# Fused attention and feed-forward on one core: one load per twin of values, all second-product tiles in pairs, halved first loads and weights, and another order

## The chip, the core and the metric

The kernel runs on one NeuronCore of a Trainium2 chip. Its engines work side by side, each through its own list of instructions in order: TensorE (PE, with its weight loads as PEld), VectorE (DVE), ScalarE (ACT), GpSimd (POOL) and SyncE (SP, which here only issues DMA transfers). They wait for each other by semaphores. The metric is the device time of one execution in microseconds (us); the median of several runs counts. Less is better.

## The reference

Cosine attention over 8 batches, 12 heads, 448 positions of 64 numbers, whose output is the input of a feed-forward layer (3584 tokens of 768 numbers, 2048 inner ones) with a hard-swish between two matrix products:

```python
q_n = q / (np.linalg.norm(q, axis=-1, keepdims=True) + 1e-06)
k_n = k / (np.linalg.norm(k, axis=-1, keepdims=True) + 1e-06)
scores = np.matmul(q_n, k_n.transpose(0, 1, 3, 2)) / tau
attn = np.exp(scores - np.max(scores, axis=-1, keepdims=True))
attn = attn / (np.sum(attn, axis=-1, keepdims=True) + 1e-09)
x = np.matmul(attn, v)            # then heads side by side: 3584 x 768
h = x @ w_in
g = h * np.clip(h + 3.0, 0.0, 6.0) / 6.0
out = g @ w_out
```

## The kernel before

**Items and twins.** An item is a pair of heads (0 to 47, six to a batch); a twin is two items. `LQ.j` loads 448 KB of q or k for a twin into the big buffer; `SQ` squares it, `RE` sums the squares, `NO` makes the inverse norms of a twin on ACT (four short instructions), `NM` normalises into bf16, `TR` transposes on PE (the first 14 loads) or `XD` by DMA (later ones). `CQ`, `CK`, `CS` copy the transposed q and k to their places. `SC.i.g` makes the scores of group g of item i (three groups of two heads, and one, M, of the 64 left-over keys of both), `EX` takes the exponential on ACT, `VA` multiplies with the values, and `FI` divides by the sum, which comes from a column of ones beside the values. `BK`, `CX` (early) or `XB`, `XP` (by DMA) bring the result transposed into xT, the input of the first product. In the first six items the scores go through two buffers of their own (SC), later through a ring of six banks of PSUM (M, Y, Z) that the products use too.

**Values.** `LV.d` (load_v) brings the values of a twin: two groups of heads and two halves of the partitions, so four transfers of 64 partitions and 128 KB each, issued one after another by SP. Chunk 3 of the keys lies half in one place and half in another, and so both halves of the partitions are loaded four chunks wide, with one chunk in both. `VC.i` (vcast) turns an item's values into bf16 with one instruction of 128 partitions and 512 elements on POOL (L355), ACT (L355) or DVE (L353).

**First product.** `F.b.f` is one of 16 units per batch: six matmuls of 448 columns (L657); `FA` and `FV` apply the hard-swish on ACT and DVE (L666, L672) into gT. The last two batches' first product is done at the end in quarters with seven products for eight (`QA` to `QV`, L1039).

**Second product.** 28 tiles of 128 tokens. Tiles (0,0) and (0,1) are done alone by four units `T` (mm2_unit, L708), each 16 matmuls of 384 columns and a move `TE`. The other 26 are taken in 13 pairs with seven products of 8 matmuls each (product_unit, L850) for the eight that two tiles would take: `G` makes sums of activations (L825), `P` multiplies, `PE` moves a product out (tokens `PE` in the plan are moves; PE in the text is TensorE), `BO` (L881, L882) and `RS` (L885) add on POOL. `WS` makes the sums of the weights once. An "a" at the end of a token `P` gives the product a bank of its own; its parts are then added by `PL`.

**Weights.** `W.n` issues a transfer on POOL's queue: w_in in four pieces (two halves of the columns, two halves of the partitions), w_out in four.

**Order.** All of it stands in one table, PLAN: a list of tokens that is run through from the start and that gives each engine its order. `DP.n` in it are n dummy matmuls of zeros (busy_pv, L1157) that keep PE at work where it has nothing else. The number at the end of a token is a part of the work, and v, p, a name the engine. Before the plan, DVE and POOL set buffers: zeros beside the values, 12 small instructions for the columns of ones (L1203 to L1205), and zeros for the dummies.

Of the kernel before, what the change touches and what calls it, by code (L numbers as in the profile page):

```python
# [120 lines left out]
def kernel(  # L121
# [62 lines left out]
    def item(n):  # L184
        return big[:, n * RAW : (n + 1) * RAW].rearrange("p (g c d) -> p g c d", g=2, c=7)

    vr = [
        big[:, c : c + VAL].rearrange("p (i c d) -> p i c d", i=4, c=5)
        for c in range((NR + 2) * RAW, (NR + 2) * RAW + NV * VAL, VAL)
    ]  # L190
    NVX = 4
    vx = [const.tile([128, 8, D + 1], BF16, name=f"vx{i}", tag=f"vx{i}") for i in range(NVX)]
    raws = [item((i + 2) % NR) for i in range(NR)]
# [441 lines left out]
    def complete(b, t):  # L635
        assert t < 3 or b - 1 in left_done

    left_done = set()
    t_read = set()

    def g_left(b, e="v"):

# [610 lines left out]
```

## Time and profile before

| | |
|---|---|
| three runs | 400.4, 402.48, 401.76 us; median 401.76 |
| the profiled execution | 399.05 us, of which span 397.3 us from the first instruction to the last |
| granted TensorE clock | 0.999 |
| matmuls | 3796 |
| HBM read, written | 47.19 MB, 11.01 MB |
| q and k, one transfer | 448 KB, median 4.5 (q) and 5.2 us (k) to land |
| values, one of four | 128 KB, median 3.6 us to land |
| w_in, one of four | 768 KB, median 13.8 us to land |

How to read the lines of the profile that follow: the page gives each engine's busy time in us, its share of the span and its count of instructions. A line of the timeline gives start, length, engine, line of the kernel, operation, target and source, a count, and in brackets the idle time before it and what ended that. The chain of waits gives the pieces of the work that ended last, in order of time. Matmuls are pipelined and their ends modelled, so "busy" on PE is not peak work.

### The profile page before, as it was taken

To read this page: it belongs to the slowest core of one execution; us is meant where nothing else is said; L and a number is where in the kernel's file an instruction comes from. 1 tells how busy PE (TensorE), PEld (TensorE's weight loads), DVE (VectorE), ACT (ScalarE), POOL (GpSimd) and SP (SyncE) were. 2 spreads that over 40 slices of the span, in tenths; PEclk is the share of its full clock that TensorE was granted. 3 is DMA by queue.
4 is the path that set the end of the run, shared out by engine and by line. 5 is a ranking of instruction groups with operands and counts; after the bars stand their busy time and mean duration, and the time that the engine had idled before them with its cause. 6 is when DMAs were issued, how large, how long until landed. Compare 5 with 4: busy or idle time off the path is not lost.

```text
span 397.3 us, 10054 instructions
## 1 busy us (share of the span) xinstructions
PE 384.8 (97%) x3796; PEld 243.4 (61%) x3796; DVE 319.0 (80%) x565; ACT 282.8 (71%) x646; POOL 289.5 (73%) x257
## 2 busy tenths in 40 slices
PE   7789999999999999999999999999999999999995
PEld 6556565555655555655655655555556579977663
DVE  6969789898897779689879468867996798988773
ACT  5898998868777777886777766786875667744310
POOL 5879865394476988588369983879764898789492
PEclk9999999999999999999999999999999999999999
DMA  8998999998989798967975697775764750011224
GB/s 286 256 269 202 236 197 299 185 152 186 228 179 244 199 235 182 233 127 187 232 177 130 173 240 195 148 173 143 124 94 123 115 91 15 2 40 41 65 63 114
DMA packets 91569, 65.35 MB, mean 164 GB/s; under 512 B 56064, under 2 KB 89984, under 8 KB 91520
## 3 DMA queue, kind: packets, MB, share of 16 engines
q1 hardware_dynamic: 87408, 58.02, 63.8%
q0 software_dynamic: 3712, 6.29, 9.0%
q8 instruction: 29, 0.48, 0.5%
q10 hardware_dynamic: 400, 0.39, 0.3%
q14 instruction: 20, 0.16, 0.1%
HBM read 47.19 MB, written 11.01 MB: 146 GB/s over the span
## 4 chain that ended last, share of the span: by engine, by line
PE 86%; DVE 5%; ACT 4%; DMA 3%; issue 1%; POOL 0%; SPq 0%; DVEq 0%; ACTq 0%
PE M L657 18%; PE M L850 15%; PE PV L522 10%; PE V L850 6%; PE M L486 6%; PE M L1039 6%; PE Z L850 5%; PE Z L657 3%; PE Y L850 3%; ACT att L505 3%; PE Y L657 3%; PE PV L1157 2%; PE Z L486 2%; PE Y L486 2%; DMA big<-in_k_dram 1%; DMA tT<-nrm 1%
## 5 line engine op out<-in xcount | busy, mean ns | idle before, releaser
L505 ACT ACTIVATE att<-M 128x448 bf16<-128x448 f32 x193 | 94.4, 561 | 15.6 <-PE M L486 12.8
L657 PE MATMUL M<-xT,w_in_sb 128*128 128x448 bf16 x414 | 86.2, 353 | 0.0
L657 PEld LDWEIGHTS <-w_in_sb 128*128 128x128 bf16 x576 | 54.3, 98 | 48.8 <-issue 2.9
L336 POOL TENSOR_TENSOR nrm<-big,r 128x896 bf16<-128x896 f32 (+1 forms) x41 | 70.3, 1722 | 18.7 <-ACT r L324 10.4
L522 PEld LDWEIGHTS <-att 128*128 128x128 bf16 (+1 forms) x1536 | 55.1, 97 | 22.5 <-issue 10.5
L522 PE MATMUL PV<-vx,att 128*128 128x65 bf16 (+1 forms) x1536 | 63.7, 193 | 0.0
L850 PEld LDWEIGHTS <-gT 128*128 128x128 bf16 x416 | 40.1, 98 | 27.1 <-issue 0.9
L305 DVE TENSOR_REDUCE n<-big 128x14 f32<-128x896 f32 (+1 forms) x50 | 51.5, 1040 | 6.2 <-ACT big L291 4.1
L293 POOL TENSOR_TENSOR big<-big 128x896 f32<-128x896 f32 (+3 forms) x25 | 41.8, 1678 | 20.1 <-DVE n L305 10.6
L672 DVE SCALAR_TENSOR_TENSOR gT<-u,M 128x448 bf16<-128x448 bf16 x69 | 41.5, 614 | 13.6 <-ACT u L666 13.1
L666 ACT ACTIVATE u<-M 128x448 bf16<-128x448 f32 x69 | 37.9, 555 | 17.8 <-PE M L657 16.4
L850 PE MATMUL M<-w_out_sb,gT 128*128 128x384 bf16 x264 | 47.3, 326 | 0.2 <-ACT att L505 0.2
L825 POOL TENSOR_TENSOR gT<-gT 128x1024 bf16<-128x1024 bf16 x12 | 28.1, 2344 | 18.0 <-DVE gs L825 17.9
L850 PEld LDWEIGHTS <-gs 128*128 128x128 bf16 x272 | 26.0, 98 | 16.4 <-issue 0.5
L543 DVE TENSOR_TENSOR on<-PV,rc 128x512 bf16<-128x512 f32 x48 | 33.2, 691 | 1.6
L486 PE MATMUL M<-tT,kz 64*128 64x448 bf16 (+1 forms) x173 | 33.3, 354 | 0.8 <-ACT att L505 0.4
L505 ACT ACTIVATE att<-Y 128x448 bf16<-128x448 f32 x52 | 29.2, 562 | 6.0 <-PE Z L486 5.4
L505 ACT ACTIVATE att<-Z 128x448 bf16<-128x448 f32 x49 | 27.6, 563 | 1.6 <-PE M L486 1.6
L442 POOL COPY km<-tT 64x128 bf16<-64x128 bf16 x34 | 15.3, 449 | 15.7 <-PE Z L486 7.7
L1039 PE MATMUL M<-xT,w_in_sb 128*128 128x224 bf16 x192 | 22.0, 259 | 0.0
L486 PEld LDWEIGHTS <-kz 64*128 64x128 bf16 (+1 forms) x296 | 13.0, 94 | 13.7 <-issue 8.8
L850 PE MATMUL M<-w_sum,gs 128*128 128x384 bf16 (+1 forms) x120 | 21.1, 321 | 0.0
(154 smaller groups left out, 748.9 us busy)
## 6 DMA issues: line engine op xcount, KB each, us to landing
big<-in_v_dram SPq DMA_DIRECT2D x96, 128.0 KB, 3.6
big<-in_q_dram SPq DMA_DIRECT2D x24, 448.0 KB, 4.5
big<-in_k_dram SPq DMA_DIRECT2D x24, 448.0 KB, 5.2
out_dram<-o SPq DMA_DIRECT2D x107, 96.0 KB, 2.2
w_in_sb<-in_moe_w_in_dram POOLq DMA_DIRECT2D x4, 768.0 KB, 13.8
w_out_sb<-in_moe_w_out_dram POOLq DMA_DIRECT2D x4, 768.0 KB, 8.5
tT<-nrm SPq DMA_TRANSPOSE x34, 4.1
xT<-on SPq DMA_TRANSPOSE x25, 3.5
```

The lines of the kernel that those rows point to most:

```text
L293: engines[e].tensor_tensor(out=o, in0=i, in1=i, op=ALU.mult)
L305: nc.vector.tensor_reduce(out=n2s[d % 2][:, j % 2, c], in_=sq[:, :, :, :].rearrange("p g c d -> p (g c) d")[:, c, :], axis=AX.X, op=ALU.add,)
L336: engines[e].tensor_tensor(out=nrm[:, :, g, :].rearrange("p c g d -> p g c d"), in0=raw_of[j][:, g, :, :], in1=rs[d % 2][3][:, j % 2, :] . ...
L486: nc.tensor.matmul(o, ks, qt[rows], start=True, stop=True)
L505: nc.scalar.activation(out=o, in_=x, func=AF.Exp, scale=inv_tau)
L522: nc.tensor.matmul(pv_out(j, h), at[rows, n, q_cols(i // HP, j)], vt[rows, 3 + h if name == "M" else 5 * h + int(name[1]), :], start=(name ...
L543: nc.vector.tensor_tensor(out=on[:, :, :, :].rearrange("p j h d -> p h j d"), in0=pv4[:, :, :, 0:D], in1=rc[:, :, :].to_broadcast([128, 2, ...
L657: nc.tensor.matmul(ps[:, 0:S], w_in_sb[:, cc, fc * 128 : (fc + 1) * 128], x[:, cc, 0:S], start=(cc == 0), stop=(cc == CC - 1),)
L666: nc.scalar.activation(out=u[:, :], in_=ps[:, 0:S], func=AF.Relu, bias=0.5, scale=1.0 / 6.0)
L672: nc.vector.scalar_tensor_tensor(out=g[:, fc, c0 : c0 + S], in0=u[:, :], scalar=1.0, in1=ps[:, 0:S], op0=ALU.min, op1=ALU.mult,)
L850: nc.tensor.matmul(m, lhs[:, c, :], rhs[:, c, c0 : c0 + width], start=(base is None and c == 0), stop=(c == KC - 1), skip_group_check=True,)
L1039: nc.tensor.matmul(o, lhs[:, c, :], rhs[:, c, :], start=start and c == 0, stop=c == KX - 1, skip_group_check=True)
```

## The change

1. The first seven twins' values come in one transfer each (128 partitions, 1,792 bytes in a piece, in the layout of q and k). Item i of the twin then lies in 64 partitions, and the cast moves each half of the chunks to its 64 partitions of vx: two instructions of 64 partitions in place of one of 128.
2. All 28 tiles are in pairs: 14 pairs, and mm2_unit is gone. Of the last three pairs, not of the last two, the sums lie in the late buffers as before (LOOP is 11 of 14 for 10 of 13).
3. w_in comes in six pieces: two quarters and a half of the columns. The first loads of q and k come in two halves (by tokens).
4. The M group always reads 64 rows (before, two of 48 read 128), so the columns of ones are set by one instruction in place of 12.
5. The table of the order is another one throughout.

```diff
-    "LQ.0 SQ.0.v.8.6 SQ.0.a.6.2 RE.0.1 LQ.1 SQ.1.p.11.3 SQ.0.a.0.6 RE.0.0 SQ.1.p.0.4 SQ.1.a.7.4 LQ.2 RE.1.1 NO.0.0 NM.0.p.0 SQ.1.a.4.3 RE.1.0 NM.0.v.1",
-    "DP.48 TR.0.Z SQ.2.a.0.7 RE.2 LQ.3 NO.0.1 NM.1.p.1 NM.1.p.0 SQ.3.a.0.7 CQ.1.v RE.3 CQ.0.a DP.12 TR.1.Y NO.1 LQ.5 SQ.5.a.0.7 CK.0.v CK.1.v SC.0.0.0",
+    "LQ.0.0 LQ.0.1 SQ.0.v.6.2 SQ.0.a.0.6 RE.0.0 SQ.0.a.8.6 RE.0.1 LQ.1.0 SQ.1.p.0.4 SQ.1.a.4.3 RE.1.0 LQ.1.1 SQ.1.v.11.3 SQ.1.a.7.4 RE.1.1 LQ.2 NO.0.0",
+    "SQ.2.a.0.7 LQ.3 NM.0.v.0 NM.0.v.1 NO.0.1 DP.23 TR.0.Z RE.2 LQ.4 LQ.5 NM.1.p.0 NM.1.p.1 SQ.3.a.0.7 RE.3 SQ.5.p.0.7 DP.10 TR.1.Y CQ.0.a CK.0.v",
...
+    VD = 7
     NVX = 4
-    vx = [const.tile([128, 8, D + 1], BF16, name=f"vx{i}", tag=f"vx{i}") for i in range(NVX)]
+    vxx = const.tile([128, NVX, 8, D + 1], BF16, name="vx", tag="vx")
+    vx = [vxx[:, i, :, :] for i in range(NVX)]
...
+        if d < VD:
+            f = v[b].rearrange("(g n) (p c) d -> n p g (c d)", g=2, c=7)[n : n + 2]
+            nc.sync.dma_start(
+                out=big[:, vr_at(d) : vr_at(d) + RAW].rearrange("p (g x) -> p g x", g=2),
+                in_=f.rearrange("n p g x -> (n p) g x"),
+            )
+            return
...
+        if i // 2 < VD:
+            for h in range(2):
+                f = big[64 * (i % 2) : 64 * (i % 2) + 64, vr_at(i // 2) + 4 * D * h : vr_at(i // 2) + 4 * D * h + 1]
+                f = bass.AP(tensor=f.tensor, offset=f.offset, ap=[f.ap[0], [6 * D, 2], [D, 4], [1, D]])
+                o = vx[i % NVX][64 * h : 64 * h + 64, :, 0:D].rearrange("p (g c) d -> p g c d", g=2)
+                if e == "v":
+                    f = f.rearrange("p g c (d x) -> p g c d x", x=1)
+                    nc.vector.tensor_reduce(out=o, in_=f, axis=AX.X, op=ALU.max)
+                else:
+                    (engines[e].copy if e == "a" else engines[e].tensor_copy)(out=o, in_=f)
+            return
...
-                    rows = slice(64 * h, 64 * h + 64) if name == "M" and halves else slice(0, 128)
+                    rows = slice(64 * h, 64 * h + 64) if name == "M" else slice(0, 128)
...
-        assert {2 * (2 * fc // FCN), 2 * (2 * fc // FCN) + 1} <= weights_in
+        assert all({2 * n, 2 * n + 1} <= weights_in for n, c in enumerate(FF) if c <= 128 * fc)
...
-    def mm2_unit(b, t, m):
...
-    TILES = [x for b in range(0, B, 2) for x in ((b, 0), (b, 1), (b, 2), (b + 1, 3), (b + 1, 0), (b + 1, 1), (b + 1, 2))][2:]
+    TILES = [x for b in range(0, B, 2) for x in ((b, 0), (b, 1), (b, 2), (b + 1, 3), (b + 1, 0), (b + 1, 1), (b + 1, 2))]
     PAIRS = list(zip(TILES[::2], TILES[1::2]))
-    LOOP = 10
+    LOOP = 11
...
-        return late_sums[n % 2][what]
+        return late_sums[(n - LOOP) % 2][what]
...
-    FG = d_ff // 2
+    FF = [0, d_ff // 4, d_ff // 2, d_ff]
     weights = [
-        (w_in_sb[64 * g : 64 * g + 64, :, f * FG : (f + 1) * FG], w_in_r[g, :, :, f * FG : (f + 1) * FG])
-        for f in range(2)
-        for g in range(2)
+        (w_in_sb[64 * g : 64 * g + 64, :, c:e], w_in_r[g, :, :, c:e]) for c, e in zip(FF, FF[1:]) for g in range(2)
     ] + [(w_out_sb[:, 4 * f : 4 * f + 4, :], w_out_r[:, 4 * f : 4 * f + 4, :]) for f in range(4)]
...
-    for t in vx:
-        nc.vector.memset(t[:, :, D : D + 1], 1.0)
-        nc.vector.memset(t[64:128, 3, D : D + 1], 0.0)
-        nc.vector.memset(t[0:64, 4, D : D + 1], 0.0)
+    nc.vector.memset(vxx[:, :, :, D : D + 1], 1.0)
```

In numbers of the plan: dummies 68 to 42 (the first run of them 48 to 23), sums of activations 65 to 70 (24 to 30 on POOL), moves of the products of pairs 92 to 99 (29 to 44 on ACT), whole or part squares on ACT 19 to 25 and on POOL 25 to 19, casts of values 10 to 13 on ACT.

Three places of the order. First ACT from the norms of the first item's k (n, ln, nr, le, r are their steps) to the first exponentials (att); tT is transposed q, big the loaded items. Before:

```order
L324 ACTIVATE r_100<-le_99 128x14
L291 ACTIVATE big<-big 128x896
L402 COPY tT_84<-Z 128x448
L321 ACTIVATE ln_101<-n_96 128x28
L322 ACTIVATE nr_102<-ln_101 128x28
L323 ACTIVATE le_103<-nr_102 128x28
L324 ACTIVATE r_104<-le_103 128x28
L291 ACTIVATE big<-big 128x896
L505 ACTIVATE att<-SC_149 128x2x448
```

and now:

```order
L329 ACTIVATE r_97<-le_96 128x14
L296 ACTIVATE big<-big 128x896
L418 COPY tT_84<-Z 128x448
L296 ACTIVATE big<-big 128x896
L326 ACTIVATE ln_98<-n_93 128x28
L327 ACTIVATE nr_99<-ln_98 128x28
L328 ACTIVATE le_100<-nr_99 128x28
L329 ACTIVATE r_101<-le_100 128x28
L418 COPY tT_84<-Z 128x448
L521 ACTIVATE att<-SC_135 128x2x448
```

The square of load 5, which stood behind the norms of the second twin, has gone to POOL, and that of load 4 has come from POOL and stands ahead of them. A second copy of q has come from DVE to stand just ahead of the exponentials.

Second, POOL in the first 35 us, from the first casts of values (CAST) on; DMA are the weights w_in, nrm the normalised items. Before:

```order
L355 CAST vx_88<-big 128x8x64
L355 CAST vx_91<-big 128x8x64
L293 TENSOR_TENSOR big<-big 128x896
L336 TENSOR_TENSOR nrm_93<-big,r_100 128x2x7x64
L336 TENSOR_TENSOR nrm_94<-big,r_100 128x2x7x64
L1146 DMA w_in_sb<-in_moe_w_in_dram 64x6x1024 x2
L293 TENSOR_TENSOR big<-big 128x896
L336 TENSOR_TENSOR nrm_92<-big,r_104 128x2x7x64
```

and now:

```order
L1131 DMA w_in_sb<-in_moe_w_in_dram 64x6x512
L363 CAST vx<-big 64x8x64 x2
L1131 DMA w_in_sb<-in_moe_w_in_dram 64x6x512
L363 CAST vx<-big 64x8x64 x4
L341 TENSOR_TENSOR nrm_90<-big,r_97 128x2x7x64
L341 TENSOR_TENSOR nrm_91<-big,r_97 128x2x7x64
L298 TENSOR_TENSOR big<-big 128x896
L341 TENSOR_TENSOR nrm_89<-big,r_101 128x2x7x64
L1131 DMA w_in_sb<-in_moe_w_in_dram 64x6x512 x2
```

The weights are issued one by one, transfers 0 and 2 ahead of the second casts, 3 and 1 behind the normalisation of load 6 (nrm_89); three casts became six instructions.

Third, POOL's end: sums of activations (gs, gT), then the adds BO (the two rows big<-big and big<-big,o in turn) and RS of the last two pairs. Before:

```order
L825 TENSOR_TENSOR gT_72<-gT_72 128x8x128
L825 TENSOR_TENSOR gs_77<-gT_72 128x1024
L881 TENSOR_TENSOR big<-big 128x384
L882 TENSOR_TENSOR big<-big,o 128x384
L881 TENSOR_TENSOR big<-big 128x384
L882 TENSOR_TENSOR big<-big,o 128x384
L885 TENSOR_TENSOR big<-big,o 128x384 x2
```

and now:

```order
L812 TENSOR_TENSOR gs_77<-gT_72 128x1024
L868 TENSOR_TENSOR big<-big 128x384
L869 TENSOR_TENSOR big<-big,o 128x384
L812 TENSOR_TENSOR gT_72<-gT_72 128x8x128
L868 TENSOR_TENSOR big<-big 128x384
L869 TENSOR_TENSOR big<-big,o 128x384
L872 TENSOR_TENSOR big<-big,o 128x384 x2
```

The sum in place (gT_72, for product 5 of pair 12) has moved behind the adds of pair 13.

More of the change, by code (lines that the diff above doesn't have):

```diff
@@ L190, with vr_at @@
     ]
+    def vr_at(d):
+        return (NR + 2) * RAW + d % NV * VAL
+    VD = 7
     NVX = 4
-    vx = [const.tile([128, 8, D + 1], BF16, name=f"vx{i}", tag=f"vx{i}") for i in range(NVX)]
+    vxx = const.tile([128, NVX, 8, D + 1], BF16, name="vx", tag="vx")
+    vx = [vxx[:, i, :, :] for i in range(NVX)]
     raws = [item((i + 2) % NR) for i in range(NR)]
@@ L269, in load_v @@
                 nc.sync.dma_start(out=o, in_=f[:, :, 3 * half * D : (3 * half + 4) * D])
-    def stagger(n):
-        assert not weights_in & {4, 5}
-        t = w_out_sb[0:8, :, :].rearrange("p f m -> p (f m)")[:, 0:4096].bitcast(FP32)
-        f = v[0, 0].rearrange("s d -> (s d)")[0 : 8 * 2048].rearrange("(p x) -> p x", p=8)
-        nc.sync.dma_start(out=t, in_=f)
     def square(j, e, c0, n):
@@ L511, in q_cols, with values @@
         return slice(128 * j, 128 * j + 128)
-    def values(i, g, rows_of="f"):
+    def values(i, g):
         needs(("VC", i), ("FI", i - 1), *([("VA", i, 0)] if g else []))
@@ L516, in values @@
         vt = vx[i % NVX]
-        halves = rows_of == "h"
         for n, name in enumerate(GROUPS[g]):
@@ L638 @@
     left_done = set()
-    t_read = set()
     def g_left(b, e="v"):
@@ L695, in out_tile @@
         return sb.tile([128, MH], FP32, name="o", tag="o", bufs=4)
-    def mm2_unit(b, t, m):
-        assert len(weights_in) == len(weights) and ("y4", "y3")[m] not in [x for x, _ in summed]
-        complete(b, t)
-        t_read.add((b, t, m))
-        if (b, t, 1 - m) in t_read:
-            g_read.add((b, t))
-        g = g_of(b)
-        ps, key = bank_of(None, 1)
-        narrow.add(key)
-        cols = slice(m * MH, m * MH + MH)
-        for fc in range(FCN):
-            nc.tensor.matmul(
-                ps[:, 0:MH],
-                g[:, fc, g_cols(b, t)],
-                w_out_sb[:, fc, cols],
-                start=(fc == 0),
-                stop=(fc == FCN - 1),
-            )
-        def store(e="a"):
-            o = out_tile()
-            moved(e, o[:, :], ps[:, 0:MH])
-            unread[key] = 0
-            result(b, t, cols, o)
-        post(f"TE.{b}.{t}.{m}", "a", store)
     LEFT, RIGHT = slice(0, MH), slice(MH, 2 * MH)
-    TILES = [x for b in range(0, B, 2) for x in ((b, 0), (b, 1), (b, 2), (b + 1, 3), (b + 1, 0), (b + 1, 1), (b + 1, 2))][2:]
+    TILES = [x for b in range(0, B, 2) for x in ((b, 0), (b, 1), (b, 2), (b + 1, 3), (b + 1, 0), (b + 1, 1), (b + 1, 2))]
     PAIRS = list(zip(TILES[::2], TILES[1::2]))
-    LOOP = 10
+    LOOP = 11
     single_read = set()
@@ L1171 @@
     OPS = {
-        "LQ": load_qk, "LV": load_v, "LS": stagger, "W": next_weights, "SQ": square, "RE": reduce, "NO": norms,
+        "LQ": load_qk, "LV": load_v, "W": next_weights, "SQ": square, "RE": reduce, "NO": norms,
         "NM": normalise, "VC": vcast, "TR": transposes, "XD": crossbar, "XB": back_crossbar, "XP": back_two, "CQ": copy_q, "CK": copy_k, "CS": copy_k3, "SC": scores,
@@ L1175 @@
         "GL": g_left, "WS": lambda x, *h: weight_sums(str(x), *((h[0] * KC // 2, KC // 2) if h else (0, KC))), "D": busy, "DP": busy_pv, "OPEN": open_ring,
-        "F": mm1_unit, "T": mm2_unit, "S": single_unit, "G": lambda x, n, e="v": g_sum(n, str(x), e), "P": product, "TB": tail_banks, "WR": wide_ring,
+        "F": mm1_unit, "S": single_unit, "G": lambda x, n, e="v": g_sum(n, str(x), e), "P": product, "TB": tail_banks, "WR": wide_ring,
         "IS": lambda x, e, *n: in_sum(str(x), e, *n), "XS": lambda b, x, *e: x_sum(b, str(x), *e), "QA": quad_first, "QB": quad_second, "QC": quad_third,
```

190 rows, old and new, of the table PLAN are left out of this document.

## The prediction

> **What bounds the kernel now.** I read the page's table of engines first, then the busy times of TensorE (PE) in four long stretches, then the chain of waits, and last the timeline of the first 45 us.
>
> ```profile
> PE 384.8 (97%) x3796; PEld 243.4 (61%) x3796; DVE 319.0 (80%) x565; ACT 282.8 (71%) x646; POOL 289.5 (73%) x257
> DMA  8998999998989798967975697775764750011224
> ...
> 40.00:100.00 60.00, 59.80 (x609) 1.00 1.06 209
> 100.00:200.00 100.00, 99.43 (x968) 1.00 0.90 204
> 200.00:300.00 100.00, 99.65 (x934) 1.00 0.71 156
> 300.00:392.00 92.00, 91.92 (x846) 1.00 0.32 66
> ```
>
> The four rows give a stretch of the span, its length and PE's busy time in it. From 40 us on PE idles 1.2 us in 352 (0.20+0.57+0.35+0.08), at the full granted clock (the 1.00). There only less matmul work makes the kernel shorter; any new wait on PE makes it longer by its whole length. Before 40 us it is otherwise:
>
> ```profile
> 2.47 7.50 PE L1157 MATMUL PV<-xT 128*128 128x248 bf16 x48 [2.47 <-DVE vx L1203]
> 9.80 0.56 PE L382 MATMUL Z<-ident,nrm 128*128 128x128 bf16 x7
> 11.47 0.55 PE L382 MATMUL Y<-ident,nrm 128*128 128x128 bf16 x7
> 12.51 0.55 PE L486 MATMUL SC<-tT,kz 64*128 64x448 bf16 x4 [0.48 <-DVE kz L404]
> ...
> 40.37 2.43 PE L657 MATMUL M<-xT,w_in_sb 128*128 128x448 bf16 x12
> ```
>
> This is PE's timeline. L1157 are the dummy matmuls; they stand in for work that isn't there yet, and the first transposes start at 9.80, when 48 of them are over. The first scores come at 12.51, and the first matmuls of the first product (L657), which fill PE from then on, at 40.37. In between PE follows the exponentials on ACT (ScalarE). So the time is: when the first product begins, plus the work behind it, plus a tail. The DMA row of the page, mean busy share of the 16 engines in slices of 9.9 us, is at 8 and 9 tenths through the first thirteen slices: early loads wait for bandwidth.
>
> **The pairs.** The four units of 16 matmuls (L708, tiles (0,0) and (0,1)) go; one pair of seven products of 8 (L850) comes in their place.
>
> ```profile
> 93.97 2.60 PE M L708 x16
> ...
> 275.29 1.30 PE Z L850 x8
> ```
>
> In the chain of waits such a unit takes 2.60 us and a product 1.30. Removed 4 x 2.60 = 10.4, added 7 x 1.30 = 9.1: **-1.3 us**, on the engine that bounds. Two groups of M that read all 128 rows become halves; that can only shorten 16 short matmuls and I count nothing for it. What a pair adds elsewhere is five sums of activations, seven moves and three adds on POOL, against four moves and their stores. In all the order has 70 such sums for 65, of which 30 instead of 24 on POOL, and 44 of the moves of the products of pairs on ACT instead of 29.
>
> ```profile
> L825 POOL TENSOR_TENSOR gT<-gT 128x1024 bf16<-128x1024 bf16 x12 | 28.1, 2344 | 18.0 <-DVE gs L825 17.9
> L610 ACT COPY o<-M 128x384 f32<-128x384 f32 x12 | 5.7, 479 | 9.3 <-DVE big L825 3.9 <-PE M L850 3.5 <-POOL km L442 1.1
> ```
>
> Six POOL sums of 2.34 are 14 us and fifteen moves of 0.48 are 7 us on engines that stand idle for over 100 us each (73% and 71% of 397). I cost them at nothing; the cover is the other products and score groups that PE does between a sum and its product. A sum that comes late by its own length costs up to 2.3 us once, since everything behind its product waits in PE's order.
>
> **The first 40 us.** Here the order counts, so I follow the rows.
>
> ```profile
> 4.44 0.72 ACT L291 ACTIVATE big<-big 128x128 f32<-128x128 f32 x2 [2.42 <-DMA big<-in_q_dram]
> 5.65 0.42 ACT L291 ACTIVATE big<-big 128x256 f32<-128x256 f32 x1 [0.49 <-DMA big<-in_k_dram]
> 7.03 0.21 ACT L324 ACTIVATE r<-le 128x14 f32<-128x14 f32 x1
> 7.32 0.94 POOL L336 TENSOR_TENSOR nrm<-big,r 128x448 bf16<-128x448 f32 x1 [0.54 <-ACT r L324]
> 7.59 0.62 DVE L305 TENSOR_REDUCE n<-big 128x7 f32<-128x448 f32 x1 [0.74 <-ACT big L291]
> 8.13 0.61 DVE L336 TENSOR_TENSOR nrm<-big,r 128x448 bf16<-128x448 f32 x1
> 10.82 0.53 ACT L402 COPY tT<-Z 128x448 bf16<-128x448 bf16 x1 [0.78 <-DVE tT L404]
> 13.56 2.94 ACT L505 ACTIVATE att<-SC 128x896 bf16<-128x896 f32 x4
> 16.38 0.25 ACT L321 ACTIVATE ln<-n 128x28 f32<-128x28 f32 x1
> 17.36 2.94 ACT L505 ACTIVATE att<-SC 128x896 bf16<-128x896 f32 x4
> ...
> 35.73 0.98 ACT L505 ACTIVATE att<-M 128x448 bf16<-128x448 f32 x2
> ...
> 12.81 0.84 ACT big L291
> 13.66 2.85 ACT att L505 x4
> ```
>
> All but the last two are of the timeline, these of the chain of waits, where overlapping ends are taken off: a whole square on ACT is 0.84, the four exponentials of an item 2.85. The second whole load lands 1.2 us behind the first (5.65 against 4.44), so a half is worth about 0.6: halves should land near 3.8, 4.4, 5.0 and 5.6. The first squares then end near 4.9, the reductions (0.6 each) near 5.75, the squares of load 1 on ACT near 6.05, and the first norms near 6.95 instead of 7.24. Both halves of load 0 are normalised on DVE, 0.6 each, done near 8.4, and only 23 dummies stand ahead of the transposes: these start near 8.45 instead of 9.80. Norms of load 1 near 8.7 after one square of 0.84; two halves on POOL of 0.94, less the overlap, end near 10.5; transposes near 10.6 instead of 11.47, scores near 11.55 instead of 12.51. ACT has as many whole squares as before ahead of the first exponentials and one copy more (0.53): square of load 4 to 10.95, norms of the second twin (about 0.9) to 11.85, that copy, so it comes to them near 12.3 instead of 13.56: 1.2 us earlier.
>
> From 13.56 to 35.73 ACT does six items of exponentials and three norms: 6 x 2.85 plus 3 x 0.98 (from 16.38 to 17.36) is 20.0 of 22.2 us. The new order puts one more square there (0.84), and its idle time lies between 0 and the same 2.1. So the first six items end between 33.2 and 35.3, against 35.73: a gain of 0.4 to 2.5. What speaks for the upper part is the loading:
>
> ```profile
> 1.26 0.45 SPq L257 DMA_DIRECT2D big<-in_k_dram  x1
> 12.80 7.20 SPq L269 DMA_DIRECT2D big<-in_v_dram  x7
> ...
> 26.64 1.67 POOL L293 TENSOR_TENSOR big<-big 128x896 f32<-128x896 f32 x1 [2.08 <-DMA big<-in_q_dram]
> ```
>
> SP stands from 12.80 to 20.0 in seven loads of values; load 8 is queued behind, and POOL waits 2.08 us for it. Now a twin is one issue (0.45 as for k) instead of four, 448 KB instead of 512, in pieces of 1,792 bytes instead of 1,024. Against it stand the casts:
>
> ```profile
> L355 POOL CAST vx<-big x25: 603/611/950, 15.4 to 319.8; 128x512 bf16<-128x512 f32 x25
> L353 DVE TENSOR_REDUCE vx<-big x13: 673/678/690, 16.9 to 282.5; 128x512 bf16<-128x512 f32 x13
> ...
> 20.00:36.00 16.00, 13.93 (x233) 9.41 (x233) 12.64 (x34) 14.14 (x26) 13.92 (x12) 1.00 0.99 239
> ```
>
> The last row gives PE, its weight loads, DVE, ACT and POOL from 20 to 36 us. Each of the first 14 becomes two of 64 partitions with the same 512 elements. No row shows one of 64 partitions with 512 elements: between 0.3 us (if time goes by partitions) and 0.61 to 0.68 (if by elements of one). I take the upper end, since all rows here go by elements: 14 more instructions, 9 us on POOL, DVE and ACT, of which six items need about half before 36 us, some 2 us on each of POOL and DVE, which have 2.1 and 3.4 of 16 us to spare there. I take **-2.0** for the whole stage, keeping -2.5 and +0.5 as bounds.
>
> **The end.**
>
> ```profile
> 382.37 0.99 POOL L881 TENSOR_TENSOR big<-big 128x384 f32<-128x384 f32 x1
> 383.44 1.33 POOL L882 TENSOR_TENSOR big<-big,o 128x384 f32<-128x384 f32 x1
> ```
>
> The last sixteen products stay sixteen. But POOL's in-place sum for product 5 of pair 12 (2.34 us) now stands behind the two adds BO of pair 13, which wait for that pair's own product 5. Counted from the last quarter-product: that product ends after four products, 5.2; its move waits on ACT behind the one of P.4.12, which ends at 6.5, so it is done near 7.6; the adds take 2.3, the sum 2.3: 12.2. PE arrives at P.5.12 after nine products, 11.7. A wait of 0.5, between 0 and 1.2; P.1.12 and all behind it are late by as much. I take **+0.4**.
>
> **Sum.** -1.3 - 2.0 + 0.4 = -2.9. The profiled execution took 399.05 (span 397.3 and 1.75 around it), so it would take 396.15. The median of the runs shown is 401.76, 2.7 above it; I carry the difference over: **398.9 us**.
>
> **Rivals.**
>
> *The start gives nothing.* The casts and the two moved steps eat the earlier start, and one or two sums or moves come late in the middle. For it: DVE and POOL are as busy as ACT before 36 us. Against it: the order leaves out 25 of 48 dummies, so earlier transposes are allowed. -1.3 + 0.4 + 0.9 = 0: 401.8.
>
> *It gives more.* The earlier values and loads also take away the waits behind 36 us, and the tail doesn't wait: -1.3 - 2.5 - 1.5 = -5.3, 396.5. Against it: after 40 us the rows show 1.2 us of idle in all, so the 1.5 has to come out of gaps that the modelled ends hide.
>
> *The weights come late (slower).* The first unit of the first product needs the first quarters of w_in, transfers 0 and 1. Transfer 1 is issued on POOL behind 3, both behind the normalisation of load 6, which needs the norms that ACT does after the third item of exponentials.
>
> ```profile
> 23.05 1.52 POOL L1146 DMA_DIRECT2D w_in_sb<-in_moe_w_in_dram  x2
> DMA to landing us min/median/max: 6.8/11.1/16.3
> ```
>
> Before, both halves needed were issued at 23.05. Now by the same sum ACT is through those norms near 12.3 + 3 x 2.85 + 2 x 0.98 + 0.84 = 23.7 to 25.8, POOL's step ends 1.7 later, and transfer 1 goes out near 28. With 6.8 to 16.3 us to land it is there between 35 and 44; PE wants it near 39. At the maximum, which was for transfers of twice the size, PE waits 5.3 us with score groups queued behind: -2.9 + 5.3 = +2.4, 404.2. It makes the kernel slower from a landing 3 us too late; at the median, 39, it costs nothing.
>
> *The clock.* PE's 48 dummies are not only filler:
>
> ```profile
> 4.00:6.00 2.00, 2.00 (x12) 1.44 (x11) 1.00 1.05 400
> 8.00:10.00 2.00, 1.97 (x19) 1.57 (x17) 1.00 1.05 376
> ```
>
> In these stretches of 2 us 12 and 19 dummies run: at the start a matmul takes nearly twice as long. With 23 dummies of 0.2 us PE works without pause until about 7.2 and then waits 1.2. If the array stays slow until the first product, each of the 24 score groups before it takes about 0.2 more (two take 0.55 in the row at 12.51, so at most 0.27 each): 4.8 us, -2.9 + 4.8 = +1.9, 403.7. The Trainium skill, "TensorE: Matmul & The Clock Gate", section "Part 1: The HAM clock gate", says that the array leaves half rate after some 3.4 us of sustained work, in a window that runs free of the kernel. By that rule 4.7 us of dummies often, not always, hold a whole window, and then the cost is nil. In the trace the change lies between the two rows, after more than 3.4 us, so it agrees as far as it goes.
>
> **Chances.** Forecast 0.50, of which 0.42 beyond 2 us of gain; more 0.12; nothing 0.20; weights late 0.12; clock 0.03; a wait in the middle that I don't see, several us, 0.03. About 0.5%, 2 us, is what a measurement of this kernel can tell from no change. Faster: 0.42 + 0.12, 0.54. Same: the rest of the forecast 0.08 and 0.17 of nothing, 0.25. Slower: 0.12 + 0.03 + 0.03 and 0.03 of nothing, 0.21. The likeliest case by itself lies at 397.3 to 400.5; the range reaches to the more-gain case and the late weights: 395.5 to 404.2, with 1 us below for the spread of the runs (400.4 to 402.48).
>
> **What would show it.** Right: the first matmuls of the first product start near 38.4 instead of 40.37, first transposes near 8.5, first exponentials near 12.3; PE busy for all but 1 to 2 us after that; no unit of 2.60 in the chain. Wrong: PE idle on w_in just before the first product (weights); first transposes early but the first product still at 40 (casts or loads: look at who waits for vx); PE idle behind POOL's or ACT's moves of the pairs between 100 and 320 us; more than 1 us of PE idle before P.5.12 in the last 15 us. The forecast falls if the first product starts later than 40.4, or if the idle time after it grows by over 2 us.

## The result and the profile after

| | median, us | lowest to highest | runs |
|---|---|---|---|
| before | 402.25 | 400.4 to 405.7 | 16 |
| after | 400.05 | 399.21 to 401.51 | 16 |

The ratio is 0.9943, with a 95% interval of 0.992 to 0.9965: 2.2 us faster, with a spread of 2.3 us instead of 5.3. The profiled execution of the change took 400.38 us (span 398.5). That is *longer* than the profiled execution of before, 399.05 (span 397.3). The two answers differ by 3.5 us, and most of this study is about those.

First the page of the changed kernel: busy time of each engine with its share and count, the granted clock of TensorE (PE) and the DMA share in slices of 10 us.

```profile
PE 384.1 (96%) x3762; PEld 239.8 (60%) x3762; DVE 309.8 (78%) x545; ACT 295.6 (74%) x670; POOL 297.7 (75%) x269
PEclk9799999999999999999999999999999999999999
DMA  7999989997898779896896597666568350012124
```

The clock shows a 7 in the second slice, which before did not have. Now the timeline of its start, PE first, then SP's issues, ACT and POOL:

```profile
2.51 4.93 PE L1142 MATMUL PV<-xT 128*128 128x248 bf16 x23 [2.51 <-DVE xT L1185]
9.09 0.56 PE L398 MATMUL Z<-ident,nrm 128*128 128x128 bf16 x7 [1.64 <-DVE nrm L341]
9.49 1.22 PE L1142 MATMUL PV<-xT 128*128 128x248 bf16 x10
12.36 0.56 PE L398 MATMUL Y<-ident,nrm 128*128 128x128 bf16 x7 [1.65 <-POOL nrm L341]
13.41 0.55 PE L502 MATMUL SC<-tT,kz 64*128 64x448 bf16 x4 [0.49 <-ACT r L329]
...
41.84 1.31 PE L671 MATMUL M<-xT,w_in_sb 128*128 128x448 bf16 x6
43.17 1.30 PE L671 MATMUL M<-xT,w_in_sb 128*128 128x448 bf16 x6
44.30 0.55 PE L398 MATMUL M<-ident,nrm 128*128 128x128 bf16 x7
44.70 1.30 PE L671 MATMUL Y<-xT,w_in_sb 128*128 128x448 bf16 x6
...
2.61 0.43 SPq L262 DMA_DIRECT2D big<-in_q_dram  x1
...
3.38 1.06 ACT L296 ACTIVATE big<-big 128x384 f32<-128x384 f32 x2 [1.36 <-DMA big<-in_q_dram]
5.66 0.36 ACT L296 ACTIVATE big<-big 128x192 f32<-128x192 f32 x1 [1.22 <-DMA big<-in_k_dram]
6.29 0.42 ACT L296 ACTIVATE big<-big 128x256 f32<-128x256 f32 x1 [0.27 <-DMA big<-in_k_dram]
8.61 0.95 ACT L296 ACTIVATE big<-big 128x896 f32<-128x896 f32 x1 [1.05 <-DMA big<-in_q_dram]
...
13.82 2.97 ACT L521 ACTIVATE att<-SC 128x896 bf16<-128x896 f32 x4
...
10.47 1.83 POOL L341 TENSOR_TENSOR nrm<-big,r 128x448 bf16<-128x448 f32 x2 [4.15 <-ACT r L329]
```

The first product (L671, before L657) starts at 41.84, not earlier than 40.37 but later. The two starts are not at the same place of the work. Before, the seven transposes of load 9 stand ahead of the first unit:

```profile
39.96 0.55 PE L382 MATMUL M<-ident,nrm 128*128 128x128 bf16 x7
```

Now they start at 44.30 (L398), and two units stand ahead of them, of 1.13 us each (43.17 to 44.30). Taken behind those transposes, less these two units, the change is at 44.70 - 2.27 = 42.43, against 40.37: **2.1 us later**. This is the common point of what follows.

What comes behind that point takes 397.3 - 40.37 = 356.9 us before and 398.5 - 42.43 = 356.1 after. So by the two profiled executions the change is 2.1 - 0.9 = 1.2 us slower, and yet its median is 2.2 us faster. The rows of PE's busy time behind 40 us (start and end, length, busy time of PE, PEld, DVE, ACT and POOL, clock, DMA share) show no idle place of note left, the tail among them:

```profile
40.00:100.00 60.00, 59.37 (x629) 32.56 (x626) 51.27 (x94) 56.08 (x135) 51.07 (x42) 1.00 0.92 202
100.00:200.00 100.00, 99.92 (x952) 58.32 (x951) 80.87 (x130) 80.61 (x187) 72.16 (x61) 1.00 0.84 199
300.00:393.00 93.00, 93.00 (x830) 69.91 (x827) 72.22 (x130) 50.11 (x111) 67.56 (x67) 1.00 0.31 64
```

### The profile page after: what moved, and what is told of

The parts are those of the page before. It is cut to its first block, busy times and chain, and to the rows that moved or that the text cites. A ratio compares the mean times of both kernels' runs of the same rounds, so it can differ in the third digit from the quotient of the medians.

```text
span 398.5 us, 9978 instructions
## 1 busy us (share of the span) xinstructions
PE 384.1 (96%) x3762; PEld 239.8 (60%) x3762; DVE 309.8 (78%) x545; ACT 295.6 (74%) x670; POOL 297.7 (75%) x269
## 3 DMA queue, kind: packets, MB, share of 16 engines
q0 software_dynamic: 4512, 6.29, 9.5%
## 4 chain that ended last, share of the span: by engine, by line
PE 85%; DVE 6%; ACT 3%; DMA 2%; issue 1%; POOL 1%; SPq 0%; DVEq 0%; POOLq 0%; ACTq 0%
PE M L671 18%; PE M L837 16%; PE PV L537 10%; PE V L837 6%; PE M L1026 6%; PE M L502 6%; PE Y L837 4%; PE Z L837 4%; PE Y L671 4%; PE Z L671 3%; PE Y L502 2%; PE Z L502 2%; DMA big<-in_q_dram 1%; DVE on L558 1%; PE Y L1026 1%
## 5 line engine op out<-in xcount | busy, mean ns | idle before, releaser
L521 ACT ACTIVATE att<-M 128x448 bf16<-128x448 f32 x193 | 95.8, 563 | 13.9 <-PE M L502 12.3
L671 PE MATMUL M<-xT,w_in_sb 128*128 128x448 bf16 x396 | 82.9, 353 | 0.0
L671 PEld LDWEIGHTS <-w_in_sb 128*128 128x128 bf16 x576 | 53.1, 98 | 46.8 <-issue 3.4
L341 POOL TENSOR_TENSOR nrm<-big,r 128x896 bf16<-128x896 f32 (+1 forms) x36 | 61.6, 1718 | 17.9 <-ACT r L329 14.5
L837 PEld LDWEIGHTS <-gT 128*128 128x128 bf16 x448 | 42.9, 98 | 28.0 <-POOL gT L812 0.8
L680 ACT ACTIVATE u<-M 128x448 bf16<-128x448 f32 x66 | 35.8, 556 | 10.8 <-PE M L671 9.7
L837 PE MATMUL M<-w_out_sb,gT 128*128 128x384 bf16 x224 | 40.4, 326 | 0.0
L298 POOL TENSOR_TENSOR big<-big 128x896 f32<-128x896 f32 (+2 forms) x19 | 31.4, 1655 | 11.7 <-DMA out_dram<-o 3.9
L812 POOL TENSOR_TENSOR gT<-gT 128x1024 bf16<-128x1024 bf16 x15 | 31.9, 2123 | 9.5 <-DVE gs L812 9.0
L837 PE MATMUL M<-w_sum,gs 128*128 128x384 bf16 (+1 forms) x192 | 34.0, 323 | 0.0
L868 POOL TENSOR_TENSOR big<-big 128x384 f32<-128x384 f32 x14 | 18.3, 1304 | 17.8 <-ACT big L625 15.0
L812 POOL TENSOR_TENSOR gs<-gT 128x1024 bf16<-128x1024 bf16 x14 | 29.7, 2123 | 2.4 <-DVE gT L686 1.2
L521 ACT ACTIVATE att<-Z 128x448 bf16<-128x448 f32 x51 | 28.6, 561 | 1.3 <-PE M L502 1.0
```

Source lines behind the costliest of these rows:

```text
L298: engines[e].tensor_tensor(out=o, in0=i, in1=i, op=ALU.mult)
L341: engines[e].tensor_tensor(out=nrm[:, :, g, :].rearrange("p c g d -> p g c d"), in0=raw_of[j][:, g, :, :], in1=rs[d % 2][3][:, j % 2, :] . ...
L521: nc.scalar.activation(out=o, in_=x, func=AF.Exp, scale=inv_tau)
L671: nc.tensor.matmul(ps[:, 0:S], w_in_sb[:, cc, fc * 128 : (fc + 1) * 128], x[:, cc, 0:S], start=(cc == 0), stop=(cc == CC - 1),)
L680: nc.scalar.activation(out=u[:, :], in_=ps[:, 0:S], func=AF.Relu, bias=0.5, scale=1.0 / 6.0)
L812: engines[e].tensor_tensor(out=o[:, :, :], in0=x, in1=y, op=op)
```

## The experiments

Medians of the kernel before that stand beside these runs: 402.95 (35 runs) for the first four, 401.92 (28) for the next four, 402.94 (18) for the last four.

**Both kernels once more.** Each unchanged, timed again and profiled again.

> The kernel before, unchanged: a second profiled execution and a control of the comparison. The two profiled executions known so far differ the other way than the medians: span 397.3 before, 398.5 after, while the medians are 402.25 and 400.05. If the first profile of before was a typical one, this span is 397 to 398 again, with the first product's matmuls (L657) starting near 40.4. If it was a lucky one, the span is 399 to 403, and the rows show where the 2 to 5 us are lost that the first profile did not show. Ratio to before 1.000 within 0.003 on either theory.

> The changed kernel, unchanged, beside the parts of it below. Theory of the prediction (earlier start, less matmul work): first product well before 40.4 in this execution. Rival (the start gives nothing or costs, and the gain is the 1.3 us of matmul work and a smaller loss elsewhere): first product at 41 to 42.5 again, and the slow matmuls between 14.7 and 21.5 us again. Ratio to before 0.992 to 0.9965.

Measured: before 402.17 us (399.67 to 406.41, ratio 0.9992 [0.9957, 1.0027]), after 399.98 (399.4 to 401.13, ratio 0.9946 [0.9912, 0.998]). The second profile of the change has a span of 397.9 and its first product at 40.99. That of before has a span of 402.2, 4.9 us more than the first, though its first product starts at 40.16. The timeline of before's second profile shows where they went, on PE, DVE, POOL and SP:

```profile
167.13 0.65 PE L522 MATMUL PV<-vx,att 128*128 128x65 bf16 x16
170.56 0.36 PE L486 MATMUL M<-tT,kz 64*128 64x448 bf16 x1 [2.78 <-DVE kz L432]
...
171.96 2.43 PE L657 MATMUL M<-xT,w_in_sb 128*128 128x448 bf16 x6
...
170.15 0.35 DVE L432 COPY kz<-tT 128x384 bf16<-128x384 bf16 x1 [3.37 <-DMA tT<-nrm]
...
170.25 0.64 POOL L442 COPY km<-tT 64x128 bf16<-64x128 bf16 x2 [3.57 <-DMA tT<-nrm]
...
164.09 3.15 SPq L393 DMA_TRANSPOSE tT<-nrm  x1
```

Near 168 us the scores of an item need transposed keys (tT) that a DMA transpose brings. It is issued at 164.09 and lands near 170; DVE's copy kz, POOL's copy km and with them PE stand. The six matmuls of the next unit then take 2.43 us instead of 1.30. PE waits 2.8 us on one transfer; the first profile of before had nothing of it. With the slow unit that is 3.9 of the 4.9 us; of the rest, PE waits 1.01 us at 117.59 for a transposed result (xT), where the first profile has 0.26.

**More dummies.** The dummy runs of the start from 23, 10 and 3 to 38, 26 and 8.

```diff
-... DP.23 TR.0.Z ... DP.10 TR.1.Y ... DP.3 SC.0.2.0 ...
+... DP.38 TR.0.Z ... DP.26 TR.1.Y ... DP.8 SC.0.2.0 ...
```

> The changed kernel with its first three runs of dummies at 38, 26 and 8 instead of 23, 10 and 3, so that PE has work in the 1.6 and 1.7 us in which it waited ahead of the first two groups of transposes. In the profile of the changed kernel matmuls ran at half speed from 14.7 to 21.5 us, some 3.5 us of work at double length. Clock theory: they run at full speed from about 7 us on, the first product starts 1 to 2.5 us earlier, ratio to the changed kernel 0.994 to 0.998. Rival (the exponentials on ACT set the start, PE has time enough): first product within 0.5 us of the changed kernel's, ratio 1.000; if the dummies overrun the transposes, up to 1 us later.

Measured: 399.5 us (398.94 to 400.83, ratio 0.9937 [0.9905, 0.997]), the clock at 1.00 throughout, the first product at 41.28, between the change's 41.84 and 40.99. The 1 to 2.5 us of the clock theory did not come: by the medians the slow clock of the start costs some 0.5 us, and it is not the main reason why the start is late.

**All values in four transfers.** The new order with the old loads and one cast an item.

```diff
-    VD = 7
+    VD = 0
```

> The changed kernel with the values of all twins in four transfers and cast by one instruction each, as before, in the new order. Theory that the single transfers relieve SP and the DMA engines: SP is held by seven more loads' worth of issues, loads 6 to 8 land 3 to 5 us later, the first product starts 1 to 3 us later, ratio to the changed kernel 1.002 to 1.008. Rival (the doubled casts cost as much as the loads give): first product within 0.7 us, ratio 0.998 to 1.002.

Measured: 406.57 us (403.01 to 409.11, ratio 1.0089 [1.0046, 1.0132]). Its timeline, SP, DVE and PE:

```profile
4.62 9.00 SPq L281 DMA_DIRECT2D big<-in_v_dram  x8
...
30.44 4.85 DVE L298 TENSOR_TENSOR big<-big 128x896 f32<-128x896 f32 x1 [0.58 <-DMA big<-in_k_dram]
...
36.19 0.94 PE L537 MATMUL PV<-vx,att 128*128 128x65 bf16 x16 [3.53 <-DVE on L558]
...
47.54 1.31 PE L671 MATMUL M<-xT,w_in_sb 128*128 128x448 bf16 x6
```

The same loads in the change:

```profile
5.08 2.29 SPq L271 DMA_DIRECT2D big<-in_v_dram  x2
...
13.27 7.52 SPq L271 DMA_DIRECT2D big<-in_v_dram  x2
```

SP stands 9.0 us in the first eight loads, where two single ones take 2.3 in the change, and the load behind them goes out at 13.75 instead of 9.09. For the next two twins the single loads hold SP no shorter (7.5 us, against 6.8 for eight). Later the square of a late key load takes DVE 4.85 us, where the change's takes 1.47; PE stands 3.53 us behind it, and the granted clock is 0.50 from 36 to 40 us. The first product starts at 47.5, later than either expectation allowed. In the new order the single transfers are worth 6.6 us; how much of that is SP's time, and why the square takes so long, was not tried.

**Single transfers in the old order.** Only the load, the casts in two parts, halves in the M group and the one instruction for the ones are taken over.

```diff
+    VD = 7
...
-    "... VA.7.3.f ..."
+    "... VA.7.3.h ..."
```

> The kernel before in its own order and with its own units, pieces of the weights and loads; only the first seven twins' values come in one transfer each, with the casts in two instructions of 64 partitions, the M group reads halves and the ones are one instruction. Theory A (what the whole change gained in the median is mostly relief of the transfers: in the kernel before they land late somewhere in the middle, by a different amount in each execution): the median falls by 1.5 to 3 us against before (ratio 0.992 to 0.996) and the spread of the timed runs, 399 to 407 before, shrinks to 3 us or less. Theory B (the gain is the pairs' 1.3 us of matmuls and the searched order; lighter transfers alone give nothing, the doubled casts cost): ratio 0.998 to 1.004 with the spread of before. In the profile: first matmuls of the first product at 39 to 40.5 by A, 40.5 to 42 by B.

Measured: 403.67 us (402.2 to 407.39), ratio 1.0042 [1.001, 1.0073]. Slower, just beyond the second theory's 1.004, and spread as before, so the first theory's number fails. The first product starts at 40.11, which tells nothing, since before has 40.37 and 40.16. What happens behind it is in the list of DMA issues from 40 to 100 us (KB each, median us to landing):

```profile
big<-in_k_dram SPq DMA_DIRECT2D x4, 448.0 KB, 8.5
...
big<-in_v_dram SPq DMA_DIRECT2D x1, 448.0 KB, 15.0
```

In the old order these are issued where they meet the weights: two pieces of w_in, issued at 42.2, take 15.8 us to land, and these loads go out meanwhile (k took 7.0 in the same stretch of before, 5.2 in the change). The lighter loads alone relieve nothing; the gain is not in them but in the order that uses them.

**w_in in the old four pieces**, at the places where quarters 0 and 1 stood.

```diff
-    FF = [0, d_ff // 4, d_ff // 2, d_ff]
+    FF = [0, d_ff // 2, d_ff]
```

> The changed kernel with w_in in the four pieces of before (two halves of the columns), at the places of the plan where the quarters 0 and 1 stood. If the quarters bring the first weights in time (theory: without them PE would wait for w_in before the first product): the first product begins 1 to 4 us later than 41 to 41.8 and the time is 1 to 4 us longer (ratio to before 0.997 to 1.004). If the weights have slack anyway: first product within 0.5 us of the changed kernel's, time within 0.8 us of 400.0.

Measured: 399.55 us (398.06 to 401.06, ratio 0.9948 [0.9917, 0.9979]), first product at 41.22. The weights have slack either way; their quarters buy nothing.

**First loads whole.**

```diff
-    "LQ.0.0 LQ.0.1 SQ.0.v.6.2 ... LQ.1.0 ... LQ.1.1 ..."
+    "LQ.0 SQ.0.v.6.2 ... LQ.1 ..."
```

> The changed kernel with the first loads of q and k whole. Step of the prediction: halves land 0.6 us earlier each and the norms begin 0.3 earlier, so without them the first transposes and all behind come 0.3 to 0.6 us later: 400.3 to 400.6. Rival (the halves only add issues: in the changed kernel's profile the two halves of k landed at 5.66 and 6.29, no earlier than the whole load of before at 5.65): first transposes earlier or equal, time 399.4 to 400.0.

Measured: 398.57 us (397.4 to 400.27, ratio 0.9902 [0.9868, 0.9937]), 1.4 below the change. The same steps in its timeline, PE first, then SP, ACT and POOL:

```profile
8.89 0.93 PE L398 MATMUL Z<-ident,nrm 128*128 128x128 bf16 x7 [1.45 <-DVE nrm L341]
9.61 2.27 PE L1142 MATMUL PV<-xT 128*128 128x248 bf16 x10
...
40.24 1.31 PE L671 MATMUL M<-xT,w_in_sb 128*128 128x448 bf16 x6
...
1.75 0.47 SPq L262 DMA_DIRECT2D big<-in_q_dram  x1
...
4.25 0.94 ACT L296 ACTIVATE big<-big 128x384 f32<-128x384 f32 x2 [2.23 <-DMA big<-in_q_dram]
5.46 0.67 ACT L296 ACTIVATE big<-big 128x192 f32<-128x192 f32 x2 [0.27 <-DMA big<-in_k_dram]
6.88 0.93 ACT L296 ACTIVATE big<-big 128x896 f32<-128x896 f32 x1
...
8.83 1.83 POOL L341 TENSOR_TENSOR nrm<-big,r 128x448 bf16<-128x448 f32 x2 [2.70 <-ACT r L329]
```

Only load 0 gains from its halves: ACT begins on the first at 3.38 and DVE on the second at 3.99, instead of both at 4.25. The halves of load 1 are there at 5.66 and 6.29, the whole one at 5.46. Two more issues on SP put load 2 back from 1.75 to 2.61, and it lands 6.0 us after its issue instead of 4.9, so 2.0 us later in all. Its square starts at 8.61 instead of 6.88, so the norms of load 1, which ACT makes behind it, come to POOL at 10.47 instead of 8.83.

**One product of four pairs twice.**

```diff
-        for c in range(KC):
+        for c in [*range(KC)] * (2 if name == "1" and 3 <= n <= 6 else 1):
```

> The changed kernel, in which product 1 of pairs 3 to 6 runs over its eight chunks twice (the repeated pass starts the sums anew, so the output is the same): 32 matmuls of 0.162 us more, 5.2 us of matmul work in the stretch from about 165 to 260 us. If PE's work sets the time there (the step on which the -1.3 us of the pairs rests): 405.2, plus 4.7 to 5.6 us. If PE only waits for others in that stretch: plus 0 to 3 us.

Measured: 404.61 us (404.31 to 405.3), 4.6 more than the change for 5.2 us of matmuls, at the lower end of the 4.7 to 5.6 expected. PE's work sets the time there.

**Lighter loads in both kernels.** From the 15th load on, only 64 of 128 partitions are brought.

```diff
-        nc.sync.dma_start(out=raw_of[j][:, g, :, :]..., in_=f[:, g, :])
+        rows = slice(0, 64) if j >= 14 else slice(0, 128)
+        nc.sync.dma_start(out=raw_of[j][rows, g, :, :]..., in_=f[rows, g, :])
```

> The kernel before, but from the 15th load of q and k on (the loads behind about 45 us) a load brings only the first 64 partitions, 224 instead of 448 KB; the other partitions keep what an earlier load left, so that half of these items are computed from old data, with the same instructions on every engine. Theory A (before loses 2 to 4 us in its typical execution because transfers land late in the middle: in three profiles its engines wait 11, 37 and (with single transfers) 17 us for transfers between 45 and 320 us, the changed kernel's 7 to 8): median 398.5 to 399.8, spread of the timed runs 3 us or less. Theory B (transfers are not what makes before slow and spread): median 401.5 to 402.5, spread as before, 4 us or more.

> The changed kernel with the same lighter loads (64 partitions from the 15th load of q and k on, half of these items from old data). Theory A: the changed kernel's order already covers its transfers, so it gains 0 to 0.7 us: 399.3 to 400.1; with that it is no faster, or even slower, than the kernel before with lighter loads. Theory B (the changed kernel has 1.3 us less matmul work and is faster by that whatever the transfers do): it stays 1.3 us or more below the kernel before with lighter loads.

Measured: before with lighter loads 398.29 us (397.31 to 399.02, ratio 0.9891 [0.9851, 0.9932]); after 399.63 (398.76 to 400.0, ratio 0.9922 [0.9896, 0.9947]). Before gains 4.6 us and loses its spread; the change gains 0.4, and is now 1.3 us *behind*. The view of the transposed q and k (tT) between 150 and 172 us ends with the time that its DMA transposes take to land. Second profile of before:

```profile
DMA to landing us min/median/max: 4.4/6.0/7.6
```

before with lighter loads:

```profile
DMA to landing us min/median/max: 2.8/3.6/4.1
```

and the changed kernel, with all its loads:

```profile
DMA to landing us min/median/max: 2.9/3.9/4.3
```

The change's transposes land there as if the traffic were halved.

**Both savings.** Whole first loads and w_in in four pieces.

> The changed kernel with whole first loads (-1.4 us when alone) and w_in in the four pieces of before (-0.4 when alone, within what can be measured). If both add: 398.0 to 398.6. If the first product then waits for the weights, because it starts earlier: 399 to 400.

Measured: 398.66 us (398.17 to 399.81, ratio 0.9903 [0.9869, 0.9938]). The two do not add; whole first loads are what counts. These two are the fastest of the kernels here that compute all of it, some 1.4 us below the change and 3.3 to 4.3 below before.

**Before, a third profile.**

> The kernel before once more, one profile, to see whether what it loses lies at one place or at a different one each time. Theory A: PE's losses beyond those of the first profile lie at another place than the 2.8 us near 170 us of the second, behind an instruction that waits for a transfer, and the other engines' waits for transfers between 45 and 320 us sum to 10 us or more. Theory B: the loss sits at 170 us again, so it is one tight place of the order.

Measured: 401.15 us, span 399.4. PE waits again, and for the same item:

```profile
168.65 0.36 PE L486 MATMUL M<-tT,kz 64*128 64x448 bf16 x1 [2.09 <-DVE kz L432]
...
168.24 0.35 DVE L432 COPY kz<-tT 128x384 bf16<-128x384 bf16 x1 [2.69 <-DMA tT<-nrm]
```

So the largest loss lies at the same tight place of the old order both times: my expectation of another place fell. That of a late transfer held, and the other engines' waits for transfers between 45 and 320 us sum to 28 us. Here the six matmuls behind the wait take 1.30 us as usual. A smaller wait lies elsewhere (0.70 us at 123.96, where the first profile has 0.22). How much of the runs up to 406 is lost here and how much elsewhere stays open: the longest execution profiled took 404.

## Why the prediction was right, and where it was not

The forecast of 398.9 us was 1.2 below the 400.05 measured and inside its own band; "faster" was the likeliest verdict. But its own condition failed (the first product not later than 40.4), so that the number came out is luck: two wrong terms cancel.

| term | predicted, us | shown, us |
|---|---|---|
| pairs | -1.3 | -0.4 to -0.9, all that lies behind the common point |
| first 40 us | -2.0 | +1.7 to +2.1 |
| tail | +0.4 | 0 |
| from the profiled execution to the median | carried over | -3.5 to -4.2 |

The ranges come from the two pairs of profiles: unchanged (+2.1, -0.9) and with lighter loads, where the common point lies at 40.16 and 44.10 - 2.27 = 41.83 and the spans are 396.4 and 397.7 (+1.7, -0.4). The last row is the gain of before from lighter loads less that of the change: 4.6 - 0.4 by the medians, and 1.09% less 0.21% of 402 us, 3.5, by the ratios.

- **The pairs.** The direction is right and PE does bound there (4.6 of 5.2 us came through). The saved 1.3 us shows to a third or two thirds. By the windows of the first two profiles PE is busy for 350.8 us behind the common point and was for 351.5, only 0.7 less; where the rest went was not looked for. The sign "no unit of 2.60 in the chain" was badly chosen: the chain groups two products into such rows too.
- **The start** is the term that failed. "Halves should land near 3.8, 4.4, 5.0 and 5.6": they were there at 3.38, 3.99, 5.66 and 6.29. The sum priced only these four pieces and left out what is queued behind them: two more issues on SP, and load 2 with the norms of the first k behind it. ACT came to the exponentials at 13.82, not 12.3. Without halves the change is 1.4 us faster. The second dummy run, which now stands ahead of the second transposes, was not followed at all: with whole loads its ten matmuls last from 9.61 to 11.88.

The rest of the lateness lies between the first exponentials and the common point, 28.6 us in the change (13.82 to 42.43) and 26.8 before (13.56 to 40.37). Here the step "its idle time lies between 0 and the same 2.1" fell. From the first exponentials to those of the seventh item (att<-M) ACT takes 24.1 us (13.82 to 37.94), and took 22.2 before (13.56 to 35.73). It is busy for 21.2 instead of 20.2, mostly the one square more that was counted, and idle for 2.95 instead of 2.02. Its two longest waits there, and a wait of PE ahead of the second one:

```profile
20.28 0.92 ACT L521 ACTIVATE att<-SC 128x896 bf16<-128x896 f32 x1 [0.93 <-PE SC L502]
37.94 0.98 ACT L521 ACTIVATE att<-M 128x448 bf16<-128x448 f32 x2 [1.42 <-PE M L502]
...
36.64 0.48 PE L1142 MATMUL PV<-xT 128*128 128x248 bf16 x3 [1.11 <-DVE on L558]
```

The first is for scores that PE makes at the low clock; the runs with more dummies and with whole loads, whose clock reads 1.00 then, do not have it. The second is there with whole loads and more dummies too, 1.42 in each: PE stands until DVE has divided an earlier item (on), and the scores that ACT needs come behind that. Before has no wait at this place.
- **The doubled casts** were rightly taken at their upper end: the time goes by the elements of a partition. The groups by form of the change (busy us, mean ns of one):

```profile
L363 POOL CAST vx<-big 64x512 bf16<-64x512 f32 x22 | 14.8, 671 | 2.6 <-issue 1.7
L371 POOL CAST vx<-big 128x512 bf16<-128x512 f32 x12 | 8.9, 745 | 0.1
```

- **The tail wait** did not come: the last row of windows above has PE busy for 93.00 of 93.00 us.
- **The step to the median** was the large mistake. The median of before stood 2.7 us above its profiled execution, and I carried that over as if it were a constant. It was a loss: late transfers, in the profiles above all the one near 168 us, by which its executions differ. The change's median lies 0.3 below its profiled execution. The change's order gives those transfers time, which is worth 3.5 to 4.2 us in the median; everything else in it, about +1.3, goes the other way. The rival "it gives more" spoke of later waits, but placed their gain in the profiled execution, where there was none to gain.
- **The weights** were not late (first product within 0.6 us with either cut), and **the clock** did fall but cost some 0.5 us, not the 4.8 of the rival.

That the new order covers its transfers is shown by the light loads and the landing times. Which of its moves does so was not tried: single moves of a table of this length were not taken apart.

## What to carry to other kernels

Where the profiled execution is faster than the median, the difference is a term with a cause: look for the transfer that lands just in time in the profile and ask what half the traffic would do, before a change is priced on that profile. Before splitting a first load, count the issues and the loads queued behind it: here only the first load gained. A lighter transfer is worth what the order makes of it: the same edit cost 1.7 us in the old order, and taking it out cost 6.6 in the new one.

## What the runs showed of the hardware

**The clock fell without a long idle time.** These windows of the changed kernel give the length, PE's busy time and count, the other engines, and, third from the end, the granted clock:

```profile
8.00:10.00 2.00, 0.91 (x12) 0.88 (x13) 1.44 (x3) 1.33 (x4) 0.00 (x0) 1.00 0.99 348
10.00:12.00 2.00, 0.71 (x7) 0.40 (x5) 1.41 (x2) 1.97 (x5) 1.53 (x2) 1.00 1.04 389
12.00:14.00 2.00, 1.15 (x12) 0.61 (x13) 1.39 (x3) 1.90 (x7) 1.74 (x2) 1.00 1.06 397
14.00:16.00 2.00, 1.35 (x7) 0.54 (x6) 2.00 (x4) 2.00 (x3) 2.00 (x3) 0.66 1.04 375
16.00:18.00 2.00, 2.00 (x14) 0.93 (x13) 1.99 (x3) 1.85 (x7) 1.94 (x4) 0.50 1.06 369
```

From 8 to 14 us PE was busy for 2.8 of 6.0 us and its longest wait was 1.65 us; then the clock went to 0.50 and stayed low until the window from 20 to 22 us. The Trainium skill, "TensorE: Matmul & The Clock Gate", section "Part 1: The HAM clock gate", has the array go back to half rate after at least one idle window of some 3.4 us. Here there was no such idle time. In the second profile of the change PE was busy for 1.9 of 4.0 us from 6 to 10, with a longest wait of 2.07, and the clock was 0.50 from 10 us on. With whole first loads it was busy for 4.4 of the 6 us from 8 to 14, with more dummies for 5.5, in before for 2.5 of the 4 us from 12 to 16, and the clock stayed at 1.00. So in these runs work at about half density lowered it, and work at three fifths or more did not. In the middle of the kernel, in the two profiles of before that wait near 168 us, the clock was 0.50 from 172 to 174.5 us behind the 2.78 us of idle and stayed at 1.00 behind the 2.09.

The prediction's other use of that page, that 4.7 us of dummies (4.93 in the change) often, not always, warm the array, agrees: in the change the seven first transposes take 0.56 us, at full rate, and with whole loads 0.93, and the ten dummies behind them 2.27 where the change needs 1.22. The granted clock reads 1.00 from 8 to 12 us in both, so at the start the length of a matmul tells the rate and the clock's row does not.

**A cast of 64 partitions takes as long as one of 128** with the same 512 elements: on POOL the medians are 614 and 612 ns. The means in the rows above, 671 and 745, hold single casts of up to 1370 and 1472 ns.

**DMA transposes of one stretch took 3.1 to 7.6 us to land** in three profiles of one program: those of tT issued between 150 and 172 us in before, 3.1 to 5.2, 4.4 to 7.6 and 3.1 to 6.5. No single profile tells that.
